# First pair of heads cast into the regrouped layout and transposed in pairs, in a windowed-attention and soft-MoE kernel

## The chip, the cores and the metric

The kernel runs on one core of one Trainium2 chip. The metric is device microseconds of one execution, the median of several runs. The core has five engines with instruction streams of their own: TensorE (PE in the profile; PEld is its weight load), VectorE (DVE), ScalarE (ACT), GpSimd (POOL) and SyncE (SP), and 16 DMA engines that move data between the main memory and the core's own memory.

## The reference

Inputs q, k and v are fp32 of shape 8 x 8 x 576 x 64 (batch, head, position, channel). The first four heads of a batch attend to a window of the last 32 positions ("plain"), the other four to every fourth of the last 128 ("dilated"). What comes out is x, 4608 rows of 512, and goes through a soft mixture of eight experts with four slots each:

```python
scores = scale * np.matmul(q, k.transpose(0, 1, 3, 2))
mask_plain = (rel >= 0) & (rel < window)
mask_dil = (rel >= 0) & (rel < window * dilation) & (rel % dilation == 0)
scores = np.where(masks[None, :, :, :], scores, -1000000000.0)
attn = softmax(scores)                      # written out in the reference
x = (attn @ v) as 4608 x 512
logits = x @ phi                            # 4608 x 32
d = softmax of logits over rows;    slot_input = d.T @ x
slot_out = relu(slot_input[e] @ w1[e]) @ w2[e]   # eight experts, four slots each
c = softmax of logits over slots;   out = c @ slot_out
```

## The kernel before

Work is cut into 32 units `u` of two heads; four units make a batch. `unit(u)` gives the batch and the pair of heads `hp`, in the order 0, 2, 1, 3: pairs 0 and 1 are plain, pairs 2 and 3 dilated. So unit 0 is heads 0 and 1, unit 1 is dilated, unit 2 is heads 2 and 3.

Loading: `load_batch(b)` brings q, k and v of a batch into one tile `home{b}` as fp16; the transfers are issued on POOL and convert on their way. Only the first two heads of q and k of batch 0 come in fp32, by the queues of SP and ACT (line 89), into the tile `stage`; VectorE casts them into `home0` (line 185, two instructions), while POOL loads heads 2 and 3 (line 186). Later the weights of an expert are loaded into the home of a batch that is done with (`load_w1`, `load_w2`, `load_half`; lines 231 to 264).

For a plain unit, q and k lie on 96 partitions with six consecutive positions each, `p (r d)`. From unit 2 on, `regroup(u)` copies the two heads on VectorE into a tile `req` or `rek` (line 280) in which the 64 channels of both heads stand side by side for each of the six positions; each of these tiles has one buffer. `transposes(u)` then turns 96x128 at a time on TensorE (line 299). For unit 0 there is no regrouping: it turns 96x64 at a time, 12 times for q and 12 for k, each into one half of the partitions (line 302). ScalarE copies the result from the accumulators into `qT` and `kTp` (line 307). Dilated units transpose straight from `home` (line 317), and VectorE writes their `kTd` (line 322).

What follows for each unit: `scores` (line 345), `softmax_parts` (exp on ScalarE, masks on VectorE), `values` (line 450, with sums), the division on VectorE (line 455), `x_transposes` (line 470), and per batch the logits, weights and slots of the mixture (`front_logits`, `front_rows`, `front_slots`). `select_v(b)` rearranges v of the plain heads by matmuls with the constant `pick` (lines 207 and 218; `pick` is made in `spread_constants`, lines 583 and 585), and `spread_v(b)` copies v of the dilated heads into `vd` (line 196). At the very start TensorE runs 14 matmuls on constant data (`warm`, line 422).

Order: POOL's instructions stand in the order written in the program. For attention, the orders on the other engines are made in advance by a planner, which follows the order of the program and its own estimates of when an instruction can start. The last stage, from the scores of the last unit on, is again in the order written, on PE, DVE and ACT: the two projections of the experts (lines 714 and 743; the last weights come in halves of columns, `SIDES`), the cast of their sum into `so` (line 798), and for each output tile a matmul (line 784), a scaling on ACT or DVE (lines 788 and 790) and a store from SP (line 793).

Of the kernel before, what the change touches and what calls it, by code (L numbers as in the profile page):

```python
# [10 lines left out]
FP16 = mybir.dt.float16  # L11
# [7 lines left out]
D = 64  # L19
# [13 lines left out]
RP, NP = 6, 96  # L33
# [26 lines left out]
def kernel(  # L60
# [10 lines left out]
    nc = tc.nc  # L71
# [13 lines left out]
    ident, mask = fixed[:, 0:128], fixed[:, 128:]  # L85
    first = {}
    for n, (nm, ten, by) in enumerate((("qp", q, nc.sync), ("kp", k, nc.scalar))):
        first[nm] = stage[0:NP, 768 * n : 768 * n + 768].rearrange("p (g x) -> p g x", g=2)
        by.dma_start(
            out=first[nm],  # L90
            in_=ten[0, 0:2].rearrange("h s d -> (h s) d").rearrange("(g p r) d -> p g (r d)", g=2, r=RP),
# [50 lines left out]
    small = ctx.enter_context(tc.tile_pool(name="small", bufs=2))  # L142
# [9 lines left out]
    ps_s = tc.alloc_tile_pool(name="ps_s", bufs=2, space=bass.MemoryType.PSUM)  # L152

    raws, w_tiles = {}, {}

    def load_batch(b):
        if b == 7:
            homes.append(big.tile([128, 8192], FP16, name="home7", tag="home7"))
        t = homes[b]
        parts = {}  # L160
        at = 0

        def load_v(nm, h0, n_h, r0, dst):
            n_p = dst.shape[0]
            dst = dst.rearrange("p (h x) -> p h x", h=n_h)
            nc.gpsimd.dma_start(  # L166
                out=dst,
                in_=v[b, h0 : h0 + n_h, r0 : r0 + 4 * n_p, :].rearrange(
                    "h (p r) d -> p h (r d)", r=4
                ),  # L170
            )
            parts[nm] = dst.rearrange("p h (r d) -> p h r d", r=4)

        for nm, ten, hs, rows in (
            ("qp", q, 0, RP), ("kp", k, 0, RP), ("qd", q, 4, RD), ("kd", k, 4, RD),
        ):
            g = 4 * S // (NP * rows)
            n = g * rows * D
            parts[nm] = t[0:NP, at : at + n].rearrange("p (g x) -> p g x", g=g)
            at += n  # L180
            src = ten[b, hs : hs + 4].rearrange("h s d -> (h s) d").rearrange(
                "(g p r) d -> p g (r d)", g=g, r=rows
            )
            if b == 0 and nm in first:
                nc.vector.tensor_copy(out=parts[nm][:, 0:2], in_=first[nm])
                nc.gpsimd.dma_start(out=parts[nm][:, 2:4], in_=src[:, 2:4])
            else:
                nc.gpsimd.dma_start(out=parts[nm], in_=src)  # L188
            if nm == "kp":
                load_v("vp", 0, 4, 0, t[:, 6144:7168])  # L190
                load_v("vt", 0, 8, 512, t[96:112, 0:2048])
        load_v("vd", 4, 4, 0, t[:, 7168:8192])
        raws[b] = parts
# [72 lines left out]
    def unit(u):  # L266
        b, i = divmod(u, 4)
        return b, (0, 2, 1, 3)[i]

    qTs, kTs, xs = {}, {}, {}  # L270

    regrouped = {}

    def regroup(u):
        b, hp = unit(u)
        if hp >= 2 or u == 0:
            return
        for nm in ("q", "k"):
            t = regrouped[nm, u] = small.tile([NP, RP, 2 * D], FP16, name=f"re{nm}{u}", tag=f"re{nm}", bufs=1)
            nc.vector.tensor_copy(  # L280
                out=t.rearrange("p r (h d) -> p r h d", h=2),
                in_=raws[b][nm + "p"][:, 2 * hp : 2 * hp + 2].rearrange("p h (r d) -> p r h d", d=D),
            )

    def transposes(u):
        b, hp = unit(u)
        for nm in ("q", "k"):
            if nm == "q":
                dst = qT_pool.tile([128, S], FP16, name=f"qT{u}", tag="qT")
                qTs[u] = dst  # L290
            else:
                dst = kTp if hp < 2 else kTd
                kTs[u] = dst
            if hp < 2:
                raw = raws[b][nm + "p"]
                rg = ring.tile([128, RP, NP], FP16, name=f"rg{nm}{u}", tag="ring")
                for r in range(RP):
                    if u > 0:
                        nc.tensor.transpose(rg[:, r, :], regrouped[nm, u][:, r], ident[0:NP, 0:NP])
                        continue  # L300
                    for h in range(2):
                        nc.tensor.transpose(  # L302
                            rg[64 * h : 64 * h + 64, r, :],
                            raw[:, 2 * hp + h, D * r : D * r + D],
                            ident[0:NP, 0:NP],
                        )
                nc.scalar.copy(  # L307
                    out=dst[:, 0:S].rearrange("c (p r) -> c p r", r=RP),
                    in_=rg.rearrange("c r p -> c p r"),
                )  # L310
            else:
                raw = raws[b][nm + "d"]
                rg = ring.tile([128, 3, 4, ND], FP16, name=f"rg{nm}{u}", tag="ring")
                for a in range(3):
                    for cc in range(2):
                        j = 2 * a + cc
                        nc.tensor.transpose(  # L317
                            rg[:, a, 2 * cc : 2 * cc + 2, :].rearrange("c h p -> c (h p)"),
                            raw[:, hp - 2, 128 * j : 128 * j + 128],
                            ident[0:NP, 0:NP],  # L320
                        )
                (nc.scalar.copy if nm == "q" else nc.vector.tensor_copy)(  # L322
                    out=dst[:, 0:S].rearrange("c (g p a) -> c g p a", g=4, a=3),
                    in_=rg.rearrange("c a g p -> c g p a"),
                )
                if nm == "k":
                    nc.vector.tensor_copy(
                        out=ends[:, :, 1:65].rearrange("p h (t a e) -> p h a t e", a=2, e=2)[:, :, :, :, 0],
                        in_=dst[:, 0:S].rearrange("p (a h t) -> p h a t", a=2, h=2)[:, :, :, 128:CL],
                    )  # L330
# [273 lines left out]
    for b in range(B):  # L604
        load_batch(b)
        if b == 0:
            nc.gpsimd.dma_start(out=phi_sb, in_=moe_phi.rearrange("(p r) s -> p r s", r=4))
    spread_constants()
    transposes(0)
    spread_v(0)  # L610
    transposes(1)
    select_v(0)
    st = scores(0)
    pr = softmax_parts(0, st)
    regroup(2)
    transposes(2)
    for u in range(NU - 2):
        st = scores(u + 1)
        if u + 3 < NU:
            regroup(u + 3)  # L620
        values(u)
        softmax_parts(u + 1, st)
        if u + 3 < NU:
            transposes(u + 3)
        b, ph = divmod(u - 4, 4)
        if b >= 0:
            if ph == 1:
                front_logits(b)
            elif ph == 2:
                front_rows(b)  # L630
            elif ph == 3:
                front_slots(b)
        if u == 1:
            spread_phi()
        if u >= 1:
            x_transposes(u - 1)
        if u % 4 == 3 and u // 4 + 1 < B:
            spread_v(u // 4 + 1)
            select_v(u // 4 + 1)
        if u % 4 == 2 and u // 4 < E_EXP - 1:  # L640
            load_w1(u // 4)
            if u // 4 < E_EXP - 3:
                load_w2(u // 4)
        if 26 <= u:
            nc.gpsimd.memset(hTp[u - 26], 0.0)
# [31 lines left out]
    for c in range(2):  # L677
# [14 lines left out]
        out=siT,  # L692
# [144 lines left out]
```

## Time and profile before

| | |
|---|---|
| Median of 3 runs | 182.64 us (182.24 to 182.81) |
| The profiled execution | 182.46 us |
| Its span, first to last instruction | 180.7 us |
| Mean granted TensorE clock | 0.912 |
| Busy: PE, PEld | 145.2 us (80%), 96.9 us (54%) |
| Busy: DVE, ACT, POOL | 124.4 us (69%), 116.1 us (64%), 53.0 us (29%) |
| Moved by the DMA engines | 41.12 MB, mean 228 GB/s |

Times in the profile's lines are microseconds from the start of the span. A line of the timeline gives start, busy time, engine, line of the program, operation, what is written from what is read (names without their buffer numbers), the shape and the count; in brackets the idle time of the engine before it and what ended it. A window's line gives for each engine busy time and number of instructions, then the granted clock of TensorE (1.00 is full speed), the mean busy share of the DMA engines, and what they moved.

### The profile page before, as it was taken

How to read it: one execution, taken by the hardware profiler on the slowest of the kernel's cores; microseconds unless marked ns; L12 is line 12 of the kernel's file. 1: busy time of each engine (PE TensorE's matmuls, PEld its weight loads, DVE VectorE, ACT ScalarE, POOL GpSimd, SP SyncE). 2: the span in 40 equal slices, each digit the busy share in tenths (PEclk: the TensorE clock that was granted, in tenths of full speed). 3: DMA queues.
4: the chain of work that ended last, by engine and by line, in shares of the span. 5: the costliest groups of instructions: out<-in, count | busy, mean ns of one | idle time of the engine just before them, and what ended most of it. 6: DMA issues, size and time to landing. Idle time of an engine off the chain costs nothing.

```text
span 180.7 us, 5164 instructions
## 1 busy us (share of the span) xinstructions
PE 145.2 (80%) x2150; PEld 96.9 (54%) x2150; DVE 124.4 (69%) x341; ACT 116.1 (64%) x216; POOL 53.0 (29%) x86
## 2 busy tenths in 40 slices
PE   6768999898989989989989889998689996886000
PEld 2324775676676567577667667665575333432000
DVE  7517699879789798798978978939731012799000
ACT  2256768987897987889789789786530313597000
POOL 7866445455554645400110040026101100000000
PEclk9985599999999999999999999999995798799755
DMA  5999999999999999999999999999999999999992
GB/s 158 189 197 202 202 202 202 202 201 204 201 206 198 204 199 204 224 214 214 216 214 219 214 218 214 219 212 214 218 216 218 203 196 175 330 391 419 432 421 122
DMA packets 29239, 41.12 MB, mean 228 GB/s; under 512 B 1696, under 2 KB 26400, under 8 KB 26784
## 3 DMA queue, kind: packets, MB, share of 16 engines
q0 software_dynamic: 24416, 30.68, 97.2%
q1 hardware_dynamic: 4592, 9.82, 14.0%
q10 hardware_dynamic: 208, 0.29, 0.6%
q8 instruction: 17, 0.28, 0.6%
q14 instruction: 6, 0.05, 0.1%
HBM read 62.02 MB, written 9.44 MB: 395 GB/s over the span
## 4 chain that ended last, share of the span: by engine, by line
PE 29%; DMA 28%; DVE 18%; ACT 9%; issue 5%; POOL 3%; DVEq 0%; ACTq 0%; POOLq 0%
DMA home<-in_moe_w_dram 24%; PE o L450 6%; DMA home<-in_v_dram 4%; ACT qT L307 4%; PE rgx L470 4%; DVE ot L790 4%; PE l L488 3%; PE sel L218 3%; ACT pr L371 3%; DVE x L455 3%; PE s L345 3%; DVE P L397 2%; PE f L784 2%; DVE kTd L322 2%; PE u L551 2%
## 5 line engine op out<-in xcount | busy, mean ns | idle before, releaser
L455 DVE TENSOR_TENSOR x<-o,rc 128x640 f16<-128x640 f32 x32 | 26.3, 821 | 0.4
L371 ACT ACTIVATE pr<-s 128x960 f16<-128x960 f32 (+1 forms) x32 | 23.0, 763 | 1.3 <-PE s L345 1.3
L378 ACT ACTIVATE pd<-s 128x640 f16<-128x640 f32 x32 | 22.0, 713 | 2.1 <-PE s L354 2.0
L166 POOL DMA_DIRECT2D home<-in_v_dram x24 | 16.5, 689 | 17.1 <-DMA home<-in_k_dram 10.0
L450 PE MATMUL o<-vd,P 128*128 128x65 f16 x256 | 14.5, 196 | 3.2 <-DVE x L455 2.6
L476 ACT COPY xT<-rgx 128x512 f16<-128x512 f16 x16 | 9.4, 590 | 10.2 <-PE rgx L470 10.2
L450 PEld LDWEIGHTS <-P 128*128 128x128 f16 x288 | 12.1, 99 | 7.1 <-DVE x L455 3.6
L231 POOL DMA_DIRECT2D home<-in_moe_w_dram x8 | 4.3, 534 | 39.6 <-PE rgq L317 31.8
L387 DVE TENSOR_TENSOR Pp<-pr,fixed 128x1280 f16<-128x1280 f16 (+1 forms) x32 | 15.5, 498 | 0.1
L790 DVE TENSOR_SCALAR ot<-f,rrow 128x256 f32<-128x256 f32 (+1 forms) x24 | 12.9, 611 | 3.8 <-PE f L784 3.8
L470 PE MATMUL rgx<-fixed,x 128*128 128x128 f16 x155 | 13.7, 219 | 1.8 <-DVE x L455 0.6
L307 ACT COPY qT<-rgq 128x576 f16<-128x576 f16 x16 | 10.2, 639 | 7.6 <-PE rgq L302 4.6
L450 PE MATMUL o<-vp,Pp 128*128 128x65 f16 x288 | 15.0, 197 | 0.0
L397 DVE TENSOR_TENSOR P<-pd,fixed 128x1024 f16<-128x1024 f16 x16 | 10.8, 677 | 4.7 <-ACT pd L378 4.7
L450 PEld LDWEIGHTS <-Pp 128*128 128x128 f16 x288 | 11.7, 100 | 4.0 <-issue 2.4
L470 PEld LDWEIGHTS <-x 128*128 128x128 f16 x160 | 10.0, 96 | 6.8 <-issue 4.4
L788 ACT ACTIVATE ot<-f,rrow 128x256 f32<-128x256 f32 (+1 forms) x24 | 12.0, 600 | 2.6 <-PE f L784 1.8
L784 PE MATMUL f<-so,ET 128*128 128x256 f16 (+1 forms) x48 | 11.1, 352 | 2.3 <-ACT ot L788 1.1
L322 DVE COPY kTd<-rgk 128x576 f16<-128x576 f16 x16 | 12.4, 773 | 0.0
L322 ACT COPY qT<-rgq 128x576 f16<-128x576 f16 x16 | 10.3, 642 | 2.8 <-PE rgq L317 2.7
L188 POOL DMA_DIRECT2D home<-in_k_dram x15 | 9.8, 654 | 6.6 <-DMA home<-in_q_dram 5.8
L215 ACT CAST vp<-sel 128x512 f16<-128x512 f32 x16 | 9.5, 596 | 3.2 <-PE sel L207 3.2
(121 smaller groups left out, 319.5 us busy)
## 6 DMA issues: line engine op xcount, KB each, us to landing
home<-in_moe_w_dram POOLq DMA_DIRECT2D x14, 1024.0 KB, 28.7
out_dram<-ot SPq DMA_DIRECT2D x5, 1024.0 KB, 9.0
home<-in_q_dram POOLq DMA_DIRECT2D x15, 288.0 KB, 9.7
home<-in_k_dram POOLq DMA_DIRECT2D x15, 288.0 KB, 10.0
home<-in_v_dram POOLq DMA_DIRECT2D x16, 256.0 KB, 9.9
out_dram<-ot SPq DMA_DIRECT2D x8, 256.0 KB, 2.9
out_dram<-ot SPq DMA_DIRECT2D x4, 512.0 KB, 8.3
home<-in_moe_w_dram POOLq DMA_DIRECT2D x2, 384.0 KB, 23.2
```

Of the source, the lines that this page charges most:

```text
L166: nc.gpsimd.dma_start(out=dst, in_=v[b, h0 : h0 + n_h, r0 : r0 + 4 * n_p, :].rearrange("h (p r) d -> p h (r d)", r=4),)
L307: nc.scalar.copy(out=dst[:, 0:S].rearrange("c (p r) -> c p r", r=RP), in_=rg.rearrange("c r p -> c p r"),)
L322: (nc.scalar.copy if nm == "q" else nc.vector.tensor_copy)(out=dst[:, 0:S].rearrange("c (g p a) -> c g p a", g=4, a=3), in_=rg.rearrange(" ...
L371: nc.scalar.activation(out=(pr[:, :, 0 : 3 * QW], pr[:, :, 3 * QW :])[part], in_=st[:, :, 0 : (480, 224)[part]], func=AF.Exp, scale=SCALE,)
L378: nc.scalar.activation(out=pr[:, part].rearrange("p c e t -> p e c t"), in_=st[:, :, 0 : 2 * DW].rearrange("p e (c t) -> p e c t", c=2), f ...
L387: nc.vector.tensor_tensor(out=Pp[:, :, b0 : b0 + nb, 0:w], in0=pr[:, :, b0 * QW : b0 * QW + nb * w].rearrange("p h (t c) -> p h t c", c=w) ...
L397: nc.vector.tensor_tensor(out=P1.rearrange("p a c t -> p (a c) t"), in0=pr[:, :, :, 0:128].rearrange("p a c t -> p (a c) t"), in1=mask[:, ...
L450: nc.tensor.matmul(ot[:, h, blk], lhs, rhs, start=(n == 0), stop=(n == len(mms) - 1), skip_group_check=True)
L455: nc.vector.tensor_tensor(out=xs[b][:, :, 2 * D * hp : 2 * D * hp + 2 * D].rearrange("p t (h d) -> p h t d", h=2), in0=ot[:, :, :, 0:D], i ...
L470: nc.tensor.transpose(rg[:, 128 * blk : 128 * blk + 128], x[:, blk, hl : hl + 128], ident)
L784: nc.tensor.matmul(fp, ET[:, c0 : c0 + 127 * nj + 1 : nj], so[:, d0:d1], start=True, stop=True)
L790: nc.vector.tensor_scalar(out=ot[:, j], in0=fp, scalar1=scale, scalar2=None, op0=ALU.mult)
```

## The change

The cast of heads 0 and 1 of batch 0 now writes the tile `req` (for q) or `rek` (for k) in the layout of the regrouped units instead of `home0`; it stays one VectorE instruction for each. `regroup` no longer makes an exception for unit 0 itself but is not called for it, and `transposes(0)` takes the path of the other plain units: six transposes of 96x128 for q and six for k in place of 12 and 12 of 96x64. The tiles' single buffers are thus used by unit 0 as well, ahead of unit 2.

```diff
--- before.py
+++ after.py
@@ -152,6 +152,11 @@
     ps_s = tc.alloc_tile_pool(name="ps_s", bufs=2, space=bass.MemoryType.PSUM)
 
     raws, w_tiles = {}, {}
+    regrouped = {}
+
+    def side_by_side(nm, u):
+        t = regrouped[nm, u] = small.tile([NP, RP, 2 * D], FP16, name=f"re{nm}{u}", tag=f"re{nm}", bufs=1)
+        return t
 
     def load_batch(b):
         if b == 7:
@@ -182,7 +187,11 @@
                 "(g p r) d -> p g (r d)", g=g, r=rows
             )
             if b == 0 and nm in first:
-                nc.vector.tensor_copy(out=parts[nm][:, 0:2], in_=first[nm])
+                t0 = side_by_side(nm[0], 0)
+                nc.vector.tensor_copy(
+                    out=t0.rearrange("p r (h d) -> p r h d", h=2),
+                    in_=first[nm].rearrange("p h (r d) -> p r h d", d=D),
+                )
                 nc.gpsimd.dma_start(out=parts[nm][:, 2:4], in_=src[:, 2:4])
             else:
                 nc.gpsimd.dma_start(out=parts[nm], in_=src)
@@ -269,14 +278,12 @@
 
     qTs, kTs, xs = {}, {}, {}
 
-    regrouped = {}
-
     def regroup(u):
         b, hp = unit(u)
-        if hp >= 2 or u == 0:
+        if hp >= 2:
             return
         for nm in ("q", "k"):
-            t = regrouped[nm, u] = small.tile([NP, RP, 2 * D], FP16, name=f"re{nm}{u}", tag=f"re{nm}", bufs=1)
+            t = side_by_side(nm, u)
             nc.vector.tensor_copy(
                 out=t.rearrange("p r (h d) -> p r h d", h=2),
                 in_=raws[b][nm + "p"][:, 2 * hp : 2 * hp + 2].rearrange("p h (r d) -> p r h d", d=D),
@@ -292,18 +299,9 @@
                 dst = kTp if hp < 2 else kTd
                 kTs[u] = dst
             if hp < 2:
-                raw = raws[b][nm + "p"]
                 rg = ring.tile([128, RP, NP], FP16, name=f"rg{nm}{u}", tag="ring")
                 for r in range(RP):
-                    if u > 0:
-                        nc.tensor.transpose(rg[:, r, :], regrouped[nm, u][:, r], ident[0:NP, 0:NP])
-                        continue
-                    for h in range(2):
-                        nc.tensor.transpose(
-                            rg[64 * h : 64 * h + 64, r, :],
-                            raw[:, 2 * hp + h, D * r : D * r + D],
-                            ident[0:NP, 0:NP],
-                        )
+                    nc.tensor.transpose(rg[:, r, :], regrouped[nm, u][:, r], ident[0:NP, 0:NP])
                 nc.scalar.copy(
                     out=dst[:, 0:S].rearrange("c (p r) -> c p r", r=RP),
                     in_=rg.rearrange("c r p -> c p r"),
```

## The prediction

> **What bounds the kernel now.** I read the page's line of DMA load and its queues first, then the chain that ended last, then the busy time by windows of five microseconds, and last the timeline at the two places that the change can reach: the first nine microseconds and the hand-over to the last stage.
>
> ```profile
> DMA  5999999999999999999999999999999999999992
> ...
> q0 software_dynamic: 24416, 30.68, 97.2%
> ...
> HBM read 62.02 MB, written 9.44 MB: 395 GB/s over the span
> ```
>
> In 38 of the 40 slices the DMA engines are busy for nine tenths of the time or more, and the queue that POOL feeds (q0) alone has packets under way for 97.2% of what 16 engines have. The chain says the same in order of time: start, duration, what.
>
> ```profile
> 5.27 7.66 DMA home<-in_v_dram
> 12.95 0.43 DVE vd L196
> ...
> 14.70 0.77 DVE kTd L322
> ...
> 29.35 0.65 ACT qT L307
> ...
> 44.30 0.65 ACT qT L307
> ...
> 102.53 0.65 ACT qT L307
> ...
> 106.37 28.66 DMA home<-in_moe_w_dram
> ...
> 140.17 15.07 DMA home<-in_moe_w_dram
> ...
> 155.29 0.41 PE sop L743 x2
> ...
> 156.27 0.83 PE f L784 x6
> ```
>
> It begins with a load of v, runs through the engines during attention, and from 106.37 on it is two transfers of expert weights, end to end but for a short issue gap; the last lands at 140.17 + 15.07 = 155.24 us. Behind it come two expert matmuls and the writing of the output. The engines in the middle of the chain do not tell whether they bind; for that I look at whether the queue of transfers ever runs empty.
>
> ```profile
> core 0: us, PE busy (x) PEld busy (x) DVE busy (x) ACT busy (x) POOL busy (x), PEclk, DMA share, GB/s
> ...
> 10.00:15.00 5.00, 3.73 (x28) 1.59 (x29) 1.98 (x7) 2.63 (x5) 3.01 (x6) 0.74 1.33 196
> 15.00:20.00 5.00, 4.37 (x54) 3.33 (x54) 2.34 (x7) 3.51 (x7) 3.03 (x5) 0.50 1.28 204
> ...
> 105.00:110.00 5.00, 4.51 (x87) 3.36 (x85) 3.99 (x11) 4.41 (x9) 2.35 (x5) 1.00 1.05 220
> ...
> 150.00:155.00 5.00, 3.62 (x30) 2.07 (x30) 2.52 (x6) 2.79 (x7) 0.00 (x0) 0.74 1.16 180
> ...
> 170.00:175.00 5.00, 0.00 (x0) 0.00 (x0) 0.00 (x0) 0.00 (x0) 0.00 (x0) 0.50 1.00 420
> ```
>
> The DMA share is 1 or more (packets of several transfers overlap) in each of these rows, in the attention stage (105 to 110) as in the writing at the end, where 420 GB/s go out while every engine is idle. The 9.44 MB of output need 9.44 / 0.420 = 22.5 us, and 155.24 + 22.5 = 177.7; the span is 180.7. So the time is a volume of transfers, loads and then stores, with little air in it. POOL's own timeline shows why a late engine does not open a hole:
>
> ```profile
> 106.37 0.53 POOL L231 DMA_DIRECT2D home<-in_moe_w_dram  x1 [14.03 <-PE rgq L317]
> ...
> 121.05 0.53 POOL L231 DMA_DIRECT2D home<-in_moe_w_dram  x1 [12.33 <-PE rgq L317]
> ...
> 140.17 0.70 POOL L264 DMA_DIRECT2D home<-in_moe_w_dram  x1 [4.04 <-DMA home<-in_moe_w_dram]
> ```
>
> POOL waited 14.03 us for a transpose of q before it could issue a weight load at 106.37 (its buffer still held q, k and v). That load landed 28.66 us later, so at the moment of issue there was about that much work still queued before it. The next issue, at 121.05 after another 12.33 us of waiting, came with 135.03 - 121.05 = 14.0 us still queued. Attention could release its buffers 14 us later than now before the queue ran dry. The issue at 140.17 waits for a landing, that is for room, not for an engine.
>
> The place where the engines are nearest to binding is the hand-over:
>
> ```profile
> 149.17 0.51 PE L743 MATMUL sop<-home,hTp 128*32 128x512 f16 x8 [0.27 <-DVE hTp L733]
> 150.59 0.40 PE L743 MATMUL sop<-home,hTp 128*32 128x256 f16 x6 [0.91 <-DMA home<-in_moe_w_dram]
> 151.31 0.29 PE L743 MATMUL sop<-home,hTp 128*32 128x256 f16 x2 [0.33 <-DMA home<-in_moe_w_dram]
> ...
> 152.06 2.43 PE L784 MATMUL f<-so,ET 128*128 128x256 f16 x12 [0.46 <-ACT so L798]
> ```
>
> TensorE has finished what it can at 149.17 + 0.51 = 149.68 and waits 0.91 us for weights, and again 0.33 us. Attention and all that follows it up to here may therefore come 0.91 + 0.33 = 1.24 us later at no cost. Coming earlier gains nothing, because the weights land when they land.
>
> **The change, part by part.** All of it lies in the first nine microseconds.
>
> ```profile
> 4.88 1.54 DVE L185 CAST home<-stage 96x768 f16<-96x768 f32 x2 [0.22 <-DMA stage<-in_q_dram]
> ...
> 6.56 1.01 POOL L188 DMA_DIRECT2D home<-in_q_dram  x1
> 6.61 0.35 DVE L280 COPY req<-home 96x768 f16<-96x768 f16 x1
> ...
> 6.62 0.45 PE L302 MATMUL rgq<-fixed,home 96*64 96x96 f16 x12
> 6.88 0.45 DVE L585 CAST pick<-stackI 128x32 f16<-128x32 f32 x4
> 6.90 0.42 PE L302 MATMUL rgk<-fixed,home 96*64 96x96 f16 x12
> ...
> 7.56 0.68 POOL L188 DMA_DIRECT2D home<-in_k_dram  x1
> ...
> 8.66 0.61 PE L207 MATMUL sel<-home,pick 32*128 32x256 f16 x14 [1.34 <-DMA home<-in_v_dram]
> ...
> 12.95 0.43 DVE L196 COPY vd<-home 128x1024 f16<-128x1024 f16 x1 [5.62 <-DMA home<-in_v_dram]
> ...
> 25.68 0.42 PE L317 MATMUL rgq<-fixed,home 96*128 96x96 f16 x6
> ...
> 25.93 0.42 PE L317 MATMUL rgk<-fixed,home 96*128 96x96 f16 x6
> ```
>
> *Matmuls.* Removed are 24 transposes of 96x64 (12 for q, 12 for k), added are 12 of 96x128. The 24 run from 6.62 to 6.90 + 0.42 = 7.32, 0.70 us. The same work in the new form is seen in the third unit of heads, also at the full clock: 25.68 to 25.93 + 0.42 = 26.35, 0.67 us for 12. So going from 24 instructions on 64 columns to 12 on 128 saves 0.03 us: the two halves of a pair lie beside each other in time already. That 0.03 us is then waited out: the next matmuls on TensorE stand at 8.66, behind the load of v that they need, 8.66 - 7.32 = 1.34 us later. If this cover were gone, the gain would be 0.03 us.
>
> *The two casts.* They stay two, of the same 768 elements for each of 96 partitions, 1.54 us together, 0.77 us each; only the order in which they are written changes, to runs of 64. Nothing in the trace shows this form from fp32. The nearest rows are the cast itself (0.77) and the fp16 copy in just this pattern (L280, 0.35). The cast runs at 768 / 0.77 = 1.0 element per ns, so I take 0.77 again; the ends are 0.35 (as the copy) and, for runs that cost extra, an estimated 1.2 (half as much again). The upper end makes the second transposes 0.9 us late, inside the 1.34 us of cover; the lower end only waits longer. Either way 0 at the end.
>
> *The regroup copy of heads 2 and 3.* It writes the tile `req`, of which there is one buffer. Before, the first unit did not use it, and the copy ran at 6.61, beside the transposes. Now it has to wait until the six transposes of q have read that tile: from 6.61 to about 6.62 + 0.45 = 7.07, so 0.46 us later. Behind it on VectorE may stand the four casts of `pick` (6.88 to 7.33), which go to 7.8 at worst; the matmuls that need `pick` start at 8.66, so 0.9 us of cover remain; a cast at its upper end uses it up, and no more. If the order places the copy after the load of v instead, it joins the chain at 12.95 (the row with 5.62 us of idle time before it), ahead of `kTd` at 14.70, and puts attention back by its own 0.35 us, which the 1.24 us at the hand-over take. For `rek` the same holds, but that copy comes after 12.95 on the chain already, 6 us behind the transposes of k, so its new wait is over before it starts.
>
> *POOL's queue.* No transfer is moved and none is added. What may shift is a collision: the issue at 6.56 took 1.01 us where its neighbour at 7.56 took 0.68, and a copy of 0.35 us on VectorE (6.61) lies inside it; 1.01 - 0.68 = 0.33. When the copy moves by 0.46 us, it hits the next issue or none, so one issue is 0.33 us earlier or another as much later. The load issued at 5.27 landed 7.66 us later, so several microseconds of transfers stand in front, and 0.33 us is no hole. The Trainium skill, "SBUF — State Buffer", section "SBUF: two separate sides", says that a VectorE operation in a mode with two ports, an fp32 copy within SBUF among them, locks POOL out while it runs, so that descriptors come late. The pair at 6.56 agrees. By that rule two casts in such a mode would hold POOL for up to 1.54 us; the sum stays as it is by the queued 7.66 us, and it would change only if the queue were empty there.
>
> Sum: -0.03 us on TensorE, 0 to +0.35 us on the chain into attention, all in front of a stage that takes 1.24 us of delay and gives nothing for being early. The profiled execution took 182.46 us (span 180.7 and 1.76 around it), 0.18 below the median of the runs, 182.64. I forecast the median unchanged, 182.6.
>
> **The rivals.** *A slower order in attention (slower).* Only POOL's order and the last stage are written out; for the rest a planner orders each engine's work in advance by its own costs, and a changed start can carry over. The mechanism would be a pattern that does not settle as well as the present one. Its price: the unit marks in the chain stand at 29.35, 44.30 and 102.53, so the first batch took 14.95 us and the four after that (102.53 - 44.30) / 4 = 14.56. If six batches ran like the first, that is 6 x 0.39 = 2.3 us; less the 1.24 us of cover, 1.1 us, so 183.7. It decides from a delay of 1.24 us at the first weights wait on. The half clock in the row of 15 to 20 us, against 1.00 later, is a second thing such a shift could prolong, by the same door. For it: the engines are busy almost throughout in attention (4.51 of 5 us on TensorE at 105), so a delay is handed on to the end. Against it: four batches in a row had the same length, so the pattern settles after one batch whatever the start was. Chance 0.19.
>
> *A better clock at the hand-over (faster).* After the waits at 150.59 and 151.31 the twelve output matmuls at 152.06 took 2.43 us, 0.20 each, where six at 156.27 took 0.83, 0.14 each; the mean clock of 150 to 155 is 0.74. If a shift of the work put them at the full clock, 12 x (0.20 - 0.14) = 0.77 us would be saved on the way to the first store, and there is a place for it in the transfers:
>
> ```profile
> 153.00:154.00 1.00, 1.00 (x6) 0.75 (x5) 1.00 (x3) 1.00 (x4) 0.00 (x0) 0.50 0.80 108
> ```
>
> This is the one slice near the end in which the DMA share falls well under 1, 0.80 and 108 GB/s. So the gain lies between 0.2 us (the air in that slice) and 0.77, and the time between 182.4 and 181.9. For it counts only that something must shift by some tenths; against it, that TensorE waits for the same weights at the same moment. The Trainium skill, "TensorE: Matmul & The Clock Gate", Part 1, has the clock follow the activity in a window of about 3.4 us that runs freely, so that the half rate would begin at another point from run to run; the trace agrees so far as it shows a granted clock of only 0.50 at 153 in the row above and 1.00 elsewhere. By that rule the shift belongs to a run as much as to the change. Chance of a gain of over 0.3%: 0.12.
>
> *A hole at the start (slower).* A POOL issue held up while the queue is still short. It would cost its length one to one, 0.33 us for a collision as seen and 1.54 for two casts, to 184.2. Against it: the load of v issued at 5.27, in the midst of the casts, landed only 7.66 us later, so the queue is no longer short by then. Chance 0.03.
>
> *It doesn't do what it says.* The matmuls are fewer by twelve, but the time on TensorE is as before (0.70 against 0.67), so the change in its own terms is empty even where it lies; that is part of the forecast and gives the same 182.6.
>
> **How the numbers follow.** 0.3% (0.55 us) is about what a measurement of this kernel can tell from no change. Unchanged, with all delays under the cover: 0.66, between 182.1 and 183.2. Slower by more: 0.19 + 0.03 = 0.22, from 183.2 to about 183.7, rarely 184.2. Faster by more: 0.12, down to 181.9. The range of 181.9 to 183.8 takes in the faster case and most of the slower one. The predicted time is that of the likeliest case.
>
> **What would show it right or wrong.** Right: 12 matmuls at line 302's place between 6.6 and 7.4 us with an end within 0.1 us of 7.3; the copy into `req` some tenths later or behind the `vd` copy; the casts at about 0.77 us; a batch still 14.56 us from mark to mark; TensorE still waiting for weights at about 150.6; the last weights landed at about 155.2. Wrong: a batch longer by a tenth or more with no wait for weights left near 150 (the slower order); the last weights landing earlier or later by over 0.5 us with the same engine work (the volume of transfers is then not what I take it for); the twelve output matmuls of the hand-over in under 2 us (the clock).

## The result and the profile after

The changed kernel takes 181.42 us (median of 6 runs, 181.12 to 181.97), the kernel before 182.72 (6 runs, 182.19 to 183.02): a ratio of 0.9923, 95% interval 0.9904 to 0.9942. It is 1.3 us faster where no change was forecast, and 181.42 lies below the range. The profiled execution took 181.12 us. All ratios here leave out disturbed runs (over 1.5% above the fastest of their kernel), while the medians do not, which matters in two of the experiments.

The page of the changed kernel, the lines that answer to those shown of before, and one more, the queue q8 (packets, megabytes, share):

```profile
span 179.4 us, 5142 instructions
...
DMA  5999999999999999999999999999999999999995
...
q0 software_dynamic: 24416, 30.68, 98.0%
...
q8 instruction: 16, 0.26, 0.5%
...
HBM read 62.02 MB, written 9.44 MB: 398 GB/s over the span
```

DMA load and bytes are as before. The span is 1.3 us shorter. One number of a line that the prediction did not look at has changed; here it is from the DMA queues of the kernel before:

```profile
q8 instruction: 17, 0.28, 0.6%
```

Queue q8 carries instructions: 17 packets before, 16 after. The chain of waits of the changed kernel:

```profile
45.73 0.65 ACT qT L305
...
60.31 0.65 ACT qT L305
...
103.96 0.65 ACT qT L305
...
107.80 27.18 DMA home<-in_moe_w_dram
...
140.13 15.06 DMA home<-in_moe_w_dram
...
155.24 0.30 PE sop L741 x2
...
156.11 0.83 PE f L782 x6
```

The last weights land at 140.13 + 15.06 = 155.19 us, 0.05 earlier than before; the output matmuls behind them begin at 156.11 where it was 156.27. So up to here at most 0.16 us are gained. What is left of the 1.3 us lies after the engines' last work, in the stores. The windows of one microsecond at the end show it, first of the kernel before, then of the changed one (the last two columns are the DMA share and GB/s):

```profile
core 0: us, PE busy (x) PEld busy (x) DVE busy (x) ACT busy (x) POOL busy (x), PEclk, DMA share, GB/s
177.00:178.00 1.00, 0.00 (x0) 0.00 (x0) 0.00 (x0) 0.00 (x0) 0.00 (x0) 0.50 0.45 180
178.00:179.00 1.00, 0.00 (x0) 0.00 (x0) 0.00 (x0) 0.00 (x0) 0.00 (x0) 0.50 0.06 25
```

```profile
177.00:178.00 1.00, 0.00 (x0) 0.00 (x0) 0.00 (x0) 0.00 (x0) 0.00 (x0) 0.50 0.36 143
178.00:179.00 1.00, 0.00 (x0) 0.00 (x0) 0.00 (x0) 0.00 (x0) 0.00 (x0) 0.50 0.00 0
```

Before, the share from 178 to 179 us is 0.06 of the 16 engines: 16 x 0.06 = 1. A single DMA engine still writes, at 25 GB/s, while the other 15 are done. After the change nothing is written in that microsecond. The packet records of the trace give the same in detail. Each engine closes its share of a transfer with a packet of 4 bytes (272 of them for the 17 stores, 17 x 16), so the end of an engine's stores can be read:

```
kernel   q8 fetches  the last one starts, lasts   end of the stores of the latest four engines (us)
before   17          161.60, 1.079                179.17  177.89  177.81  177.68 ...
after    16          148.62, 0.945                177.88  177.63  177.55  177.50 ...
```

A packet of q8 is read here as a fetch of TensorE's instructions: it has 16,384 bytes and comes once in 250 or so of them. Before, the seventeenth came at 161.60, in the midst of the stores, when 4282 of the 4307 instructions in TensorE's records had begun. It took 1.08 us, and one engine ends 179.17 - 177.89 = 1.28 us later than the next. (A packet of 4 bytes at 177.92 belongs to the late engine itself: it closes that engine's share of the transfer before the last, and eight packets of 4096 bytes follow it without a gap.) The records do not name the engines, so that the late engine is the one that fetched is inferred. The changed kernel has 4283 instructions in the records, 24 fewer (12 matmuls and their 12 weight loads), and ends without a seventeenth fetch; the records do not show at which instruction it would have come.

The front of the changed kernel, from its timeline:

```profile
4.62 0.89 POOL L197 DMA_DIRECT2D home<-in_k_dram  x1
...
4.82 0.56 DVE L191 CAST req<-stage 96x768 f16<-96x768 f32 x1
...
5.29 0.57 DVE L191 CAST rek<-stage 96x768 f16<-96x768 f32 x1
...
5.86 0.42 PE L304 MATMUL rgq<-fixed,req 96*128 96x96 f16 x6
...
6.12 0.42 PE L304 MATMUL rgk<-fixed,rek 96*128 96x96 f16 x6
...
6.31 0.35 DVE L287 COPY req<-home 96x768 f16<-96x768 f16 x1 [0.18 <-PE rgq L304]
...
8.19 0.61 PE L216 MATMUL sel<-home,pick 32*128 32x256 f16 x13 [1.65 <-DMA home<-in_v_dram]
...
13.16 0.43 DVE L205 COPY vd<-home 128x1024 f16<-128x1024 f16 x1 [6.12 <-DMA home<-in_v_dram]
```

The transposes run from 5.86 to 6.54 us, 0.68 us for 12. The copy into `req` waits for them and runs at 6.31. Then everything waits for v as before, TensorE to 8.19 and VectorE to 13.16.

### The profile page after: what moved, and what is told of

Its sections match the earlier page's. It is cut to its first block, busy times and chain, and to the rows that moved or that the text cites. A ratio compares the mean times of both kernels' runs of the same rounds, so it can differ in the third digit from the quotient of the medians.

```text
span 179.4 us, 5142 instructions
## 1 busy us (share of the span) xinstructions
PE 145.9 (81%) x2138; PEld 98.0 (55%) x2138; DVE 124.1 (69%) x341; ACT 116.2 (65%) x216; POOL 52.9 (30%) x86
## 3 DMA queue, kind: packets, MB, share of 16 engines
HBM read 62.02 MB, written 9.44 MB: 398 GB/s over the span
## 4 chain that ended last, share of the span: by engine, by line
PE 30%; DMA 28%; DVE 17%; ACT 9%; issue 5%; POOL 3%; DVEq 0%; ACTq 0%; POOLq 0%
DMA home<-in_moe_w_dram 24%; PE o L448 6%; DMA home<-in_v_dram 4%; PE rgx L468 4%; ACT qT L305 4%; DVE ot L788 4%; PE sel L227 3%; PE l L486 3%; ACT pr L369 3%; PE s L343 3%; DVE x L453 3%; DVE P L395 2%; PE f L782 2%; DVE kTd L320 2%; PE u L549 2%
## 5 line engine op out<-in xcount | busy, mean ns | idle before, releaser
L315 PEld LDWEIGHTS <-home 96*128 96x128 f16 x192 | 10.4, 103 | 3.3 <-DMA home<-in_q_dram 2.0
## 6 DMA issues: line engine op xcount, KB each, us to landing
home<-in_moe_w_dram POOLq DMA_DIRECT2D x2, 384.0 KB, 22.5
```

## The experiments

Two theories. **F (fetch):** the gain is the seventeenth block of TensorE's instructions, which is no longer fetched during the stores. **W (front work):** it comes from the new casts and the start of attention. In all runs of before beside these the median was between 182.7 and 182.9 us. The last two columns of the table are from the packet records of each profiled execution: by how much the last engine ends its stores after the next to last, and the time from the last packet of weights to the last packet of a store.

| run | median us | ratio to before, 95% interval | fetches | last fetch starts | last engine late by | weights to stores |
|---|---|---|---|---|---|---|
| before | 182.72 | | 17 | 161.60 | 1.28 | 24.23 |
| after | 181.42 | 0.9923 [0.9904, 0.9942] | 16 | 148.62 | 0.24 | 22.95 |
| after_again | 181.09 | 0.9914 [0.9898, 0.9929] | 16 | 148.21 | 0.33 | 22.95 |
| narrow_from_regrouped | 182.71 | 0.9995 [0.998, 1.001] | 17 | 161.75 | 1.45 | 24.40 |
| after_more_warm | 182.62 | 0.9995 [0.998, 1.001] | 17 | 162.24 | 1.48 | 24.30 |
| after_6_more_warm | 182.83 | 0.9996 [0.9984, 1.0008] | 17 | 167.60 | 1.50 | 24.45 |
| before_12_left_out_late | 181.51 | 0.9926 [0.9912, 0.9939] | 16 | 146.74 | 0.28 | 22.95 |
| before_100_more | 182.02 | 0.9957 [0.9941, 0.9973] | 17 | 149.50 | 0.30 | 22.95 |
| before_50_late | 182.01 | 0.9953 [0.9936, 0.997] | 17 | 154.76 | 0.05 | 23.17 |
| after_load_one_engine | 182.02 | 0.9956 [0.9941, 0.9971] | 16 | 147.20 | 0.42 | 23.37 |
| after_load_16_engines | 181.59 | 0.9932 [0.9912, 0.9951] | 16 | 147.57 | 0.30 | 23.00 |

**One part undone: narrow transposes from the regrouped tiles.**

```diff
                 for r in range(RP):
-                    nc.tensor.transpose(rg[:, r, :], regrouped[nm, u][:, r], ident[0:NP, 0:NP])
+                    if u > 0:
+                        nc.tensor.transpose(rg[:, r, :], regrouped[nm, u][:, r], ident[0:NP, 0:NP])
+                        continue
+                    for h in range(2):
+                        nc.tensor.transpose(
+                            rg[64 * h : 64 * h + 64, r, :],
+                            regrouped[nm, u][:, r, D * h : D * h + D],
+                            ident[0:NP, 0:NP],
+                        )
```

> The changed kernel with one part undone: the casts still write the regrouped tiles, but unit 0 is transposed by 24 transposes of 96x64 again, so TensorE has as many instructions as before the change. Theory F (fetch): the gain is the 17th block of TensorE's instructions, whose 16 KB transfer of 1.08 us at 161.60 us lay on one DMA engine during the stores; it comes back with the count: 17 blocks, one of them between 155 and 178 us, the last store packet near 179.2 us, 182.7 us. Theory W (front work): the gain is the faster casts (0.56 for 0.81 us) and the start of attention; they stay, so 181.4 us with the last store packet near 177.9.

Measured 182.71 us: the whole gain is gone, though the new casts and their tiles stay. Its queues and its end:

```profile
q8 instruction: 17, 0.28, 0.6%
```

```profile
177.00:178.00 1.00, 0.00 (x0) 0.00 (x0) 0.00 (x0) 0.00 (x0) 0.00 (x0) 0.50 0.71 291
178.00:179.00 1.00, 0.00 (x0) 0.00 (x0) 0.00 (x0) 0.00 (x0) 0.00 (x0) 0.50 0.07 29
```

The seventeenth packet is back, and with it the late engine: the next to last ends at 178.25, the last at 179.70 (hence 0.07 and 29 GB/s in the second row). W falls: the casts took 0.56 and 0.57 us here, as in the changed kernel, and gave nothing.

**The same number of instructions taken away elsewhere, in the kernel before.**

```diff
         for n, (_, c0, nj) in enumerate(cols):
+            if b >= B - 2:
+                break
             nc.tensor.matmul(
                 ep[:, 10, n : n + 1], ET[:, c0 : c0 + 127 * nj + 1 : nj], quarter, start=True, stop=True
             )
+        if b >= B - 2:
+            nc.vector.memset(ep[:, 10, 0 : len(cols)], 1.0)
```

> The kernel before with its front untouched; left out are the twelve one-column matmuls that sum the weights of the last two batches (lines 538, at about 131.6 and 145.5 us), in whose place VectorE writes ones, so the rows of these batches are scaled wrongly. TensorE has 24 instructions fewer, as in the change, and nothing before 131 us differs. Theory F: 16 blocks of instructions, no fetch after 155 us, the whole gain: 181.5 us beside 182.8 for the kernel before. Theory W: 182.8 us.

Measured 181.51 us, the full gain, without any part of the change. (It leaves out twelve sums, so the rows of two batches come out wrong.) The queue and the end:

```profile
q8 instruction: 16, 0.26, 0.5%
```

```profile
177.00:178.00 1.00, 0.00 (x0) 0.00 (x0) 0.00 (x0) 0.00 (x0) 0.00 (x0) 0.50 0.84 344
178.00:179.00 1.00, 0.00 (x0) 0.00 (x0) 0.00 (x0) 0.00 (x0) 0.00 (x0) 0.50 0.01 4
```

This is the run that settles it: the order of all other instructions is that of the kernel before, and up to 131 us the program is the same.

**As many added elsewhere, in the changed kernel.** `warm(14, heat)` becomes `warm(9, heat)` and `warm(17, heat[:, 0:128])`.

> The changed kernel with 26 warm-up matmuls (9 of 512 columns and 17 of 128) in place of 14 of 512, about as long in time: twelve more matmuls, all done before the first transposes. Theory F: the 17th block is back, 182.7 us. Theory W: the change itself is whole, so 181.4 us.

Measured 182.62 us; the gain is gone. And half as many, `warm(13, heat)` and `warm(7, heat[:, 0:128])`:

> The changed kernel with six more warm-up matmuls (13 of 512 columns and 7 of 128 in place of 14 of 512), twelve instructions: half of the way back. Theory F: either the boundary of the 17th block is passed, and the whole 1.3 us is back (182.7 us), or it isn't, and nothing is (181.4 us); it cannot be half. A theory in which each instruction costs something: half of the gain, 182.05 us.

Measured 182.83 us. Twelve instructions more bring back the whole loss:

```profile
177.00:178.00 1.00, 0.00 (x0) 0.00 (x0) 0.00 (x0) 0.00 (x0) 0.00 (x0) 0.50 0.56 229
178.00:179.00 1.00, 0.00 (x0) 0.00 (x0) 0.00 (x0) 0.00 (x0) 0.00 (x0) 0.50 0.06 25
```

So it is a step and not a price for each instruction. The boundary lies between 12 and 24 instructions below the count of the kernel before. The fetch came at 167.60 us here, later than in the other runs, and cost as much. This run also shows best what the fetch takes away: from 165.6 to 167.6 us and again in the 2 us behind the fetch 16.1 to 16.2 store packets are under way on average, and during its 0.93 us 15.1, one fewer.

**More matmuls than before, and faster.** 100 more, at the start: `warm(2, heat)` and 112 matmuls of 32 columns.

> The kernel before with 100 more matmuls at the start: 2 of 512 columns and 112 of 32 in place of 14 of 512. Theory F: 17 blocks as before, but each is reached 200 instructions earlier, so the last is fetched near 147 us, ahead of the stores, and the 18th is not reached: 181.4 to 181.9 us, faster than the kernel before though it has 100 matmuls more. Theory W, and any theory in which the number of matmuls itself costs time: 182.7 us or more.

Measured 182.02 us, 0.8 us faster than the kernel before with 100 matmuls more, and a little above the 181.4 to 181.9 expected. That agrees with F in kind: the last engine is late by only 0.30 us and the stores take 22.95 us after the weights. But only 0.8 of the 1.3 us are gained. In the profiled execution the last engine ended its weights at 155.61 us, 0.81 after the next (154.81); in the changed kernel at 154.93, 0.24 after. A fetch at 149.50 that puts one engine back on the weights would explain it; the changed kernel, with a fetch at 148.62, does not show it. The weights also landed late where the whole gain was measured: at 155.31 us in `before_12_left_out_late`, at 155.74 in `after_load_16_engines`. So the missing 0.5 us stay open.

**The fetch at the seam of loads and stores.** 50 matmuls of 32 columns into a spare accumulator, behind `expert_out(6, chs=range(HALF))`.

> The kernel before with 50 extra matmuls of 32 columns at the hand-over, where TensorE waits for weights at about 149.7 us; nothing ahead of that differs. 17 blocks, the last reached 100 instructions earlier, near 156 to 157 us instead of 161.6, at the start of the stores. Theory F in its plain form: any fetch during the stores costs the same, 182.8 us. Theory F with a bound of supply: until 162 us the stores come at 384 GB/s, under what the engines move later, so the engine catches up, and most of the 1.3 us is gained: 181.6 to 182.1 us, with the last store packet within 0.6 us of the one before it. The extra matmuls themselves take about 1.4 us where 0.91 + 0.33 us are waited, so up to 0.3 us may be added.

Measured 182.01 us. The fetch came at 154.76, a little before it was expected, and the reason given is not what the profile shows:

```profile
149.83 1.35 PE L766 MATMUL spare<-fixed 128*32 128x32 f16 x48
...
151.73 0.29 PE L743 MATMUL sop<-home,hTp 128*32 128x256 f16 x2 [0.15 <-DMA home<-in_moe_w_dram]
...
155.02 0.40 PE L743 MATMUL sop<-home,hTp 128*32 128x256 f16 x6 [0.32 <-DMA home<-in_moe_w_dram]
...
156.81 0.40 PE L743 MATMUL sop<-home,hTp 128*32 128x256 f16 x2 [1.39 <-DMA home<-in_moe_w_dram]
```

The last two expert matmuls wait 1.39 us for weights: the last packet of them ended at 156.07 us, about 1.1 later than in before (154.94), and 0.7 after the next engine (155.36). The last seven packets of 512 bytes begin at 155.72, as the fetch (154.76 to 155.73) ends. So the engine that fetched was, it seems, late with the weights and not with the stores, and then the last two engines end 0.05 us apart. The profiled execution was the slowest of the six (182.51 us). Whether an engine could catch up among the stores stays open.

**The disputed cost by itself.** One extra load of 16 KB during the stores of the changed kernel, on ScalarE's queue, first into one partition and then, as 16 rows of 1 KB, into 16.

```diff
     for i in range(FIRST_TILES, len(OUT_TILES)):
+        if i == FIRST_TILES + 1:
+            nc.scalar.dma_start(
+                out=homes[4][0:1, :].bitcast(FP32),
+                in_=moe_w1[0, 0:4].rearrange("(o r) f -> o (r f)", o=1),
+            )
         finish_tile(i, 0, DMODEL)
```

> The changed kernel with one extra load of 16 KB from the main memory into one partition of a dead buffer, issued by ScalarE during the stores (about 161 us): an imitation of the lost fetch. Theory F: if the 16 KB fall to one DMA engine, that engine ends about 1.0 us behind the others, 182.4 us. A theory in which the number of bytes or the extra transfer as such counts gives +0.04 us (16 KB at 420 GB/s), 181.4 to 181.5.

> The same 16 KB as 16 rows of 1 KB into 16 partitions. Theory F: spread over the engines, it delays each by less than 0.1 us: 181.5 us, at most 0.1 above the changed kernel, and about 0.9 below the run with one partition. The theory of bytes: the same time in both runs.

Measured 182.02 us with one partition and 181.59 with 16, on one chip: 0.43 us apart, and the intervals overlap at their ends ([0.9941, 0.9971] and [0.9912, 0.9951]). In the profiled execution, the fastest of its runs (181.43 us), the single packet took 0.81 us, and the last engine ended 0.42 us after the next. The sign is that of F, the size half of what was expected, so this pair leans to F and does not show it. The runs with one partition range from 181.43 to 182.65. An engine that would have ended up to 0.6 us before the last (177.30 to 177.88 in the changed kernel) has that much room, so the delay would depend on which engine takes the packet; the records do not name the engine, and this was not tried further.

**Runs in which something else moved.** Three more tried to change the count at the start of the kernel before.

> The kernel before, with its casts and its 24 narrow transposes, but with 2 warm-up matmuls in place of 14: twelve fewer matmuls in another place. Leaves out no part of the result. Theory F: 16 blocks of instructions, none after 155 us, 181.4 us. Theory W: nothing gained, 182.7 us, or more since TensorE starts colder.

> The kernel before, with two fp32 warm-up matmuls of 512 columns in place of 14 fp16 ones: at least 24 instructions of TensorE fewer, but a warm-up that should be nearly as long (an fp32 matmul counted as four passes), so that the start is not colder. Casts, 24 narrow transposes and order as before. Theory F: 16 blocks of instructions, none fetched after 155 us, 181.4 us (on a chip where the kernel before takes 182.7). Theory W: 182.7 us. If the start is colder all the same, attention comes late by more than the cover at the hand-over, and the time is higher by that.

> The kernel before with 50 more matmuls at the start (2 of 512 columns and 62 of 32 in place of 14 of 512): 17 blocks, the last reached 100 instructions earlier, near 155 to 158 us, just as the stores begin. Theory F in its plain form, any fetch after the loads costs its 1.1 to 1.3 us: 182.8 us. Theory F with a bound of supply: until 162 us the stores move 384 GB/s, under the 410 to 440 of later, so an engine that falls behind early can catch up, and a part or all of it is gained: 181.6 to 182.3 us. Theory W: 182.8 us or more.

Measured 184.38, 183.21 and 183.89 us, ratios 1.0052 [1.0023, 1.0081], 1.0025 [1.0003, 1.0047] and 1.0044 [1.0013, 1.0075]. All three expectations under F missed, and so they can't be counted for it. In these three the planner also put other work in another order (of the 341 places in VectorE's order 20, 31 and 20 hold another instruction than before; in `before_100_more` and `before_50_late` none), and so they no longer test one thing. Why the first and the third are slower was not followed. With the fp32 warm-up, the one of the three followed in its profile, TensorE waited for the casts of `pick`, and reached the first output matmuls at 155.48 us instead of 152.06:

```profile
13.88 1.03 PE L208 MATMUL sel<-home,pick 32*128 32x256 f16 x7 [6.73 <-DVE pick L586]
```

```profile
154.28 0.73 PE L744 MATMUL sop<-home,hTp 128*32 128x512 f16 x16 [0.27 <-DVE hTp L734]
...
155.48 2.01 PE L785 MATMUL f<-so,ET 128*128 128x256 f16 x12 [0.48 <-ACT so L799]
```

There is no wait for weights left in front of the expert matmuls at 154.28. This is the slower rival of the prediction, seen where it was not looked for.

## Why the prediction was wrong

**The step that failed is in the bound: "9.44 / 0.420 = 22.5 us, and 155.24 + 22.5 = 177.7; the span is 180.7".** It set the volume of stores against their rate and let the 3.0 us to the end of the span pass as a remainder. Of these, 1.28 us (177.89 to 179.17) were a single DMA engine at work on its own, which the row for 178 to 179 us of the windows shows (0.06, 25 GB/s); 1.5 us more lie between the last packet and the end of the span, in both kernels. "The time is a volume of transfers" was right, but the sum took the mean of 16 engines, and the end comes with the last of them.

**With it failed the price of the transposes: "So going from 24 instructions on 64 columns to 12 on 128 saves 0.03 us".** It priced an instruction by its time on TensorE. On the path that sets the end it counted as part of a transfer of 16 KB: 24 instructions fewer, and one block less to load. What TensorE gained at the front is waited out in front of v as forecast (1.65 us of wait before 8.19); the measured gain, 1.3 us, came by another way, and no term of the sum stood for it. The line that held it, q8 with 17 packets, stood on the page. The Trainium skill, "Runtime: NRT & Kernel Launch", section "Instruction fetch mechanics", has instructions loaded in blocks of 16 KiB, 256 at a time, over a DMA queue of the engine's own, with a cost at each boundary that is mostly hidden. The traces agree on the size and nearly on the spacing, (4282 - 243) / 16 = 252 recorded instructions between fetches. "Mostly hidden" does not hold for the one in the stores, with which the kernel takes 1.3 us more (182.7 for 181.4); what each of the others costs, no run here shows by itself.

**What held.** The matmuls: 0.68 us for the 12 after the change, 0.67 forecast, though with the shorter casts they end at 6.54 and not near 7.3. The copy into `req` was forecast 0.46 us later; it runs behind the transposes as forecast, but these came so early that it starts 0.30 us earlier than before (6.31 for 6.61), and no wait followed from it. The cover at the hand-over was put to the test unasked. In the profiled execution the clock of TensorE was low for a stretch between 30 and 40 us (mean 0.66 in both windows):

```profile
30.00:35.00 5.00, 4.81 (x60) 3.46 (x60) 3.42 (x10) 3.95 (x8) 2.39 (x4) 0.66 1.35 200
35.00:40.00 5.00, 5.00 (x65) 3.71 (x63) 4.53 (x13) 4.01 (x8) 3.03 (x5) 0.66 1.28 204
```

Attention came 45.73 - 44.30 = 1.43 us later, and the hand-over of the changed kernel reads:

```profile
150.89 0.73 PE L741 MATMUL sop<-home,hTp 128*32 128x512 f16 x16 [0.27 <-DVE hTp L731]
...
152.09 2.01 PE L782 MATMUL f<-so,ET 128*128 128x256 f16 x12 [0.48 <-ACT so L796]
...
154.56 0.40 PE L741 MATMUL sop<-home,hTp 128*32 128x256 f16 x6 [0.24 <-DMA home<-in_moe_w_dram]
...
155.24 0.29 PE L741 MATMUL sop<-home,hTp 128*32 128x256 f16 x2 [0.28 <-DMA home<-in_moe_w_dram]
```

Here the 16 expert matmuls start 150.89 - 149.17 = 1.72 us later than before, and the first output matmuls at 152.09, only 0.03 us later. The waits of 0.91 and 0.33 us are gone, which is the cover of 1.24 us worked out in the prediction; the rest is that the 16 matmuls, now without waits among them, take 0.73 us where their three pieces took 0.51 + 0.40 + 0.29 = 1.20. And the last weights landed where they were forecast.

**The casts** took 0.56 and 0.57 us, not 0.77, below the value taken and inside its bounds. It has no effect on the end that can be seen: `after_load_16_engines` has the same casts at 0.76 and 0.83 us and the gain all the same (181.59 us), and `narrow_from_regrouped` has the short ones and no gain. The casts of `after_load_16_engines`:

```profile
4.89 0.76 DVE L191 CAST req<-stage 96x768 f16<-96x768 f32 x1 [0.23 <-DMA stage<-in_q_dram]
...
5.58 0.83 DVE L191 CAST rek<-stage 96x768 f16<-96x768 f32 x1
```

**The rivals.** The faster one, a better clock at the hand-over, had the right sign for the wrong reason, which is luck: the twelve output matmuls did run faster (2.01 for 2.43 us), but the first store did not gain by it, 153.08 us after and 153.05 before. The slower one did not occur with the change: on VectorE, ScalarE and POOL all instructions stand in the same order in both kernels, and attention took (103.96 - 45.73) / 4 = 14.56 us for a batch, as before.

## What to carry to other kernels

When the end is set by transfers, look at the last microseconds by windows of one: a DMA share of one sixteenth is one engine that is late, and then ask what only that engine had to carry. The stream of instructions is a transfer too; in a kernel like this one a few instructions fewer can drop a whole block, and the gain belongs to where the last block is fetched and not to the place where the instructions were saved: 24 fewer at another place gained as much, and 100 matmuls more gained 0.8 us. So before a small gain is put down to what was changed, take the same number of instructions away somewhere else.

## What was not expected of the hardware

A fetch of TensorE's instructions took 0.89 to 1.20 us for 16 KB (1.47 once). In the four kernels in which one came well among the stores, between 161.6 and 167.6 us, one engine ended 1.28 to 1.50 us after the next; this does not follow the length of the fetch (1.50 with 0.93 us, 1.45 with 1.47), and what adds to it was not followed. At 167.6 us TensorE's stream had all but ended (4292 of 4295 recorded instructions had begun), and the block was fetched nonetheless. The same cast of 96x768 from fp32 took 0.56 to 0.57 us in four executions and 0.73 to 0.83 in three others; POOL's issue beside it took 0.88 to 0.92 us in those four and 0.63 to 0.64 in those three, so it looks as if one of the two waits for the other; no run isolates it.
